# Strassen's identity for the second matrix product of the last 1024 tokens, with a transposed output and weight sums kept in DRAM

## The chip, the cores and the metric

One core of a Trainium2 chip runs the kernel. The metric is the device time of one execution in microseconds (us): 905.93 us before the change (median of three runs, 903.33 to 907.97). TensorE (PE) does the matrix products, VectorE (DVE), ScalarE (ACT) and GpSimd (POOL) the elementwise work, and SyncE (SP) issues nearly all DMAs. Each engine works through its own instructions in order.

## What is computed

```
out_up    = np.repeat(softmax_attention(q_d, k_d, v_d), 4, axis=2)   # means of 4 positions
out_local = softmax_attention(q, k, v, mask |i-j| < 4)
x = (out_up + out_local) as [4608 tokens, 512]
h = x @ w_in                                # w_in  512 x 2048
g = h * np.clip(h + 3.0, 0.0, 6.0) / 6.0
out = g @ w_out                             # w_out 2048 x 512
```

There are 8 batches of 576 positions, so 4608 tokens. The two products are called GEMM1 (with `w_in`) and GEMM2 (with `w_out`). Each 32-bit operand is split into a rounded high part and a rest, and a product is three matmuls: high by high, high by low, low by high. "To round a tile" below means the two instructions that make the parts: one copy (`hi`, mostly ACT) and one subtraction (`lo`, mostly DVE).

## The kernel before

The attention of a batch leaves its part of x in the arena, a large buffer in on-chip memory. The MoE part runs over chunks of 512 tokens (`PART`, nine of them). For chunks 0 to 6 `plan_moe` does GEMM1 block by block (f = 0 to 15, 128 of the 2048 hidden columns each, L1067) and GEMM2 two blocks behind (L1126, accumulated in four PSUM banks o0 to o3, a bank for 128 tokens). While chunk n runs, the attention of the batches of chunk n+1 is worked in between, mostly on DVE, ACT and POOL.

The last two chunks are one piece of 1024 tokens (`plan_strassen`, called with n = `PAIR0` = 7). Their GEMM1 goes by Strassen's identity: for each of eight groups of two hidden blocks, `plan_group` makes sums of the quarters of the weights (`whole` L1333, `mix` L1340, rounded at L1354 and L1357) and seven products P1 to P7 of six matmuls each (L1370) in place of eight. A bank called "chain" takes P1, then P6, P7 and P5 on top, and is copied by ACT in between (L1386); DVE adds the other banks (L1403), and relu and gate follow (L1413, L1417). Their GEMM2 is plain: `plan_parts` rounds each gated tile (L1442 on ACT, L1446 on DVE or POOL) and `gemm2` (L1460) multiplies it. The first chunk's GEMM2 stands between the products of the groups, the second's follows behind all groups. The last tiles leave PSUM in halves (L1032 on ACT, L1034 on DVE) and are stored in pieces of 2 KB rows (L1038) on the queues of SP and ACT.

The order of the instructions is no hand-written list. Every piece of work is declared with `op` (engines and costs, what it waits for, the buffers it takes and frees, a due time `dl`), and `Plan.emit` simulates the engines with a table of costs and writes out each engine's instructions in that order. A lower due time goes first. Work that may go to DVE or POOL goes by cost and by a penalty (`PEN`); with `lock=True` the plan never lets the two run such work at once. On the chip the order is fixed, and only semaphores hold instructions back.

Of the kernel before, what the change touches and what calls it, by code (L numbers as in the profile page):

```python
# [8 lines left out]
F32 = mybir.dt.float32  # L9
# [9 lines left out]
DM, DFF = 512, 2048  # L19
# [37 lines left out]
def tile_local_down_attention_moe(ctx, tc, q_all, k_all, v_all, _qk_loc, _v_loc, w_in, w_out, ident_d, _mask_d, out):  # L57
# [900 lines left out]
    def plan_split(n, prev_last):  # L958
# [3 lines left out]
        def part(i, k, off, cnt):  # L962
            return parts_of(n)[i][:, k:k + ks, off:off + cnt]

        def hi(eng, b, s0, off, cnt, k):
            copy_on(eng, part(0, k, off, cnt), x_of(n, b, k, ks, s0, cnt))

        def lo(eng, b, s0, off, cnt, k):
            eng.tensor_tensor(
                part(1, k, off, cnt), x_of(n, b, k, ks, s0, cnt), part(0, k, off, cnt).bitcast(F32),  # L970
                op=ALU.subtract)
# [36 lines left out]
    def plan_store(n, m, ready, frees):  # L1008
# [9 lines left out]

        def store():
            for p, k, first in stores(at, P):  # L1020
# [4 lines left out]
        if n == len(PART) - 1:  # L1025

            def ev_half(i, eng):
                if i == 0:
                    st_o[n, m] = buf("obz", (n, m), [P, DM])
                cs = slice(i * DM // 2, (i + 1) * DM // 2)  # L1030
                if eng is nc.scalar:
                    eng.activation(st_o[n, m][:, cs], otile[n, m][:, cs], AF.Copy, scale=1.0 / 6.0)  # L1032
                else:
                    eng.tensor_scalar(st_o[n, m][:, cs], otile[n, m][:, cs], 1.0 / 6.0, None, op0=ALU.mult)  # L1034

            def store_half(i, eng):
                for p, k, first in list(stores(at, P))[i::2]:
                    eng.dma_start(  # L1038
                        bass.AP(tensor=out.tensor, offset=out.offset + first, ap=[[32 * DM, k], [1, DM]]),
                        st_o[n, m][p:p + k])  # L1040

            e = [op("ACT", 0.37, partial(ev_half, 0, nc.scalar), [ready], take=[("obz", (n, m))], free=[frees])]
            e.append(op("DVE", 0.37, partial(ev_half, 1, nc.vector), [ready] + e, take=[("obz", (n, m))], free=[frees]))
            op("SP", 1.2, partial(store_half, 0, nc.sync), e, free=[("obz", (n, m))], size=dma(P, 1024), nd=3)
            op("ACT", 1.0, partial(store_half, 1, nc.scalar), e, free=[("obz", (n, m))])
            return
# [3 lines left out]
    def plan_moe(n):  # L1050
# [6 lines left out]
        for f in range(NF):  # L1057
# [49 lines left out]
            read_w[f] = a  # L1107
# [9 lines left out]
        for f in range(NF):  # L1117
# [16 lines left out]
            if f < NF - 1:  # L1134
                before = gemm2
            after = st["ready"] + [w_done["o", f]]
            if n == len(PART) - 1 and f == NF - 2:
                continue
            if n == len(PART) - 1 and f == NF - 1:

                def last_two(m, a=gemm2, b=before):
                    b(m)
                    a(m)

                ops_ = []
                for m in range(parts):
                    ops_.append(op(
                        "PE", 2 * cost, partial(last_two, m), after + gs[f - 1]["ready"] + [w_done["o", f - 1]] + prev[-1:], dl=dl,
                        rec=6))
                    prev.append(ops_[-1])  # L1150
                for key_ in ("gh", "gl"):
                    plan.free_after((key_ + k0, (key_, (n, f - 1))), ops_)
            elif f == 0 or f == NF - 1:
# [27 lines left out]

    def plan_strassen(n, prev_last):

        t0 = start_of(n)
        half = NK // 2
        places = {}
# [17 lines left out]
        def raw_x(t, kh, off, cnt):  # L1204
            b, s0 = divmod((n + t) * TOK + off, S)
            return xt[b][:, kh * half:(kh + 1) * half, s0:s0 + cnt]

        def cuts(*ts):

            at = {0, TOK}  # L1210
            for t in ts:
                at |= {S * b - (n + t) * TOK for b in range(B) if 0 < S * b - (n + t) * TOK < TOK}
            at = sorted(at)
            return [(a, b - a) for a, b in zip(at, at[1:])]

        def ready_x(t, kh, off, cnt):
            b = ((n + t) * TOK + off) // S
            return [x for h in range(kh * half, (kh + 1) * half) for x in x_done[b, h]]
# [3 lines left out]
        def reads(t, off, o):  # L1222
            readers.setdefault(((n + t) * TOK + off) // S, []).append(o)
# [6 lines left out]
        def split(name, source, deps, users, t=None, kh=None):  # L1230

            his, los = [], []
            for off, cnt in cuts(t) if t is not None else [(0, TOK)]:
                def of(off=off, cnt=cnt):
                    return raw_x(t, kh, off, cnt) if t is not None else source()

                def hi(eng, off=off, cnt=cnt, of=of):
                    copy_on(eng, xpart(name, 0)[:, :, off:off + cnt], of())

                def lo(eng, off=off, cnt=cnt, of=of):  # L1240
                    eng.tensor_tensor(xpart(name, 1)[:, :, off:off + cnt], of(),
                                      xpart(name, 0)[:, :, off:off + cnt].bitcast(F32), op=ALU.subtract)

                d = list(deps) + (ready_x(t, kh, off, cnt) if t is not None else [])
# [3 lines left out]
                his.append(a)  # L1248
                los.append(c)
                if t is not None:  # L1250
                    reads(t, off, a)
                    reads(t, off, c)
# [5 lines left out]
        def combine(name, a_of, b_of, deps, cut, frees=()):  # L1258

            got = []  # L1260
            for off, cnt in cut:
                def sub(eng, off=off, cnt=cnt):
                    eng.tensor_tensor(tmp(name)[:, :, off:off + cnt], a_of(off, cnt), b_of(off, cnt), op=ALU.subtract)
                got.append(op(on("xlo", half * cnt), 0, sub, deps(off, cnt), take=[("xT", name)], lock=True))
            return got

        def of_tmp(name):
            return lambda off, cnt: tmp(name)[:, :, off:off + cnt]

        def of_x(t, kh):  # L1270
            return lambda off, cnt: raw_x(t, kh, off, cnt)
# [3 lines left out]
        t1 = combine("t1", of_x(1, 0), of_x(0, 0), lambda o, c: ready_x(1, 0, o, c) + ready_x(0, 0, o, c), cuts(0, 1))  # L1275
        t2 = combine("t2", of_x(1, 1), of_tmp("t1"), lambda o, c: t1 + ready_x(1, 1, o, c), cuts(1))
        split("t2", lambda: tmp("t2"), t2, [])
        t3 = combine("t3", of_x(1, 1), of_x(1, 0), lambda o, c: ready_x(1, 1, o, c) + ready_x(1, 0, o, c), cuts(1))
        split("t3", lambda: tmp("t3"), t3, ["t3"])
        t4 = combine("t4", of_x(0, 1), of_tmp("t2"), lambda o, c: t2 + ready_x(0, 1, o, c), cuts(0))  # L1280
# [12 lines left out]
        loaded, prods, s_free = {}, {}, {}  # L1293
# [4 lines left out]
        def weight(i, j, part, kk):  # L1298
# [7 lines left out]
            pair_, row = {6: (0, 0), 7: (0, 1), 3: (1, 0), 5: (1, 1)}[j]  # L1306
            return sums(part)[:, pair_, row, ks]

        def sums(part):
            return spare(4 + part).rearrange("p k t -> p (k t)").rearrange("p (a r n) -> p a r n", a=2, r=2)  # L1310

        MOVING = {1: "b11", 2: "b21", 3: "b22", 4: "t4", 5: "t1", 6: "t2", 7: "t3"}
        gs = {}

        def plan_group(i):

            at = t0 + GROUP * i
# [11 lines left out]
            def whole(x, eng):  # L1329
                if x == 0:  # L1330
                    st["w"] = buf("wf", i, [P, 2, 512])
                w = blocks(i)[x].bitcast(F32)
                eng.tensor_tensor(st["w"][:, x], w[:, 0], w[:, 1], op=ALU.add)  # L1333

            def mix(k, eng):
                u = st["w"].rearrange("p r (a n) -> p r a n", a=2)
                a11, a12, a21, a22 = u[:, 0, 0], u[:, 0, 1], u[:, 1, 0], u[:, 1, 1]
                out_, x, y, o = ((a22, a21, a22, ALU.add), (a21, a11, a21, ALU.subtract),
                                 (a11, a22, a11, ALU.subtract), (a12, a12, a11, ALU.subtract))[k]
# [686 lines left out]
```

## Time and profile before

| | before |
|---|---|
| median of three runs | 905.93 us |
| the profiled execution | 904.18 us |
| its span, first to last instruction | 902.0 us |
| PE busy in the span | 883.8 us |
| DVE, ACT, POOL busy | 592.2, 472.5, 237.5 us |
| moved by DMA | 106 MB |

The span is shorter than the execution by 2.18 us, which lie outside the first and last instruction. In the rows of the profile "L1460" is line 1460 of the kernel, "PEld" the loading of weights into PE (beside the matmuls), "SPq" and "ACTq" the queues that issue DMAs, and the numbers at the end of a group of instructions are its busy time and the mean of one in ns.

### The profile page before, as it was taken

Reading aid. Unit: us, or ns where it says so; the run is one execution under the profiler, and the core shown is the slowest. Engines: PE = TensorE matmul, PEld = TensorE weight load, DVE = VectorE, ACT = ScalarE, POOL = GpSimd, SP = SyncE. Lnnn points to the kernel's source line nnn. Section 1 sums busy time; section 2 is a strip of 40 time slices with the busy share of each in tenths; the row PEclk is TensorE's granted clock in tenths of the full one; section 3 lists DMA queues with packets and bytes.
Section 4 is the critical chain, followed back from the end, with each engine's and each line's share of the span. In section 5 each row is a group of like instructions: output and inputs, shape, how many; then the busy total and the mean of one; then the engine's idle time right before and its main releaser. Section 6 shows DMA issues by size and latency. Waiting matters only on the chain.

```text
span 902.0 us, 19402 instructions
## 1 busy us (share of the span) xinstructions
PE 883.8 (98%) x6961; PEld 722.2 (80%) x6961; DVE 592.2 (66%) x1073; ACT 472.5 (52%) x1511; POOL 237.5 (26%) x316
## 2 busy tenths in 40 slices
PE   6999999999999999999999999999999999999997
PEld 5667788788888888888888888888888888888886
DVE  7898876466776766656666665666655868766422
ACT  5798866455655455555454535455552334444421
POOL 3655542044522132123211330223110222000000
PEclk9999999999999999999999999999999999999999
DMA  9999843366666663655365546777541022210011
GB/s 227 276 236 235 193 125 70 94 123 120 125 130 125 133 134 72 131 111 114 80 144 103 108 88 136 196 174 190 134 112 36 1 78 86 70 70 24 13 36 47
DMA packets 315759, 106.08 MB, mean 118 GB/s; under 512 B 251792, under 2 KB 298000, under 8 KB 315664
## 3 DMA queue, kind: packets, MB, share of 16 engines
q1 hardware_dynamic: 314384, 103.09, 49.7%
q10 hardware_dynamic: 1280, 1.76, 0.6%
q8 instruction: 55, 0.90, 0.4%
q14 instruction: 40, 0.33, 0.1%
HBM read 75.89 MB, written 28.90 MB: 116 GB/s over the span
## 4 chain that ended last, share of the span: by engine, by line
PE 90%; DMA 3%; DVE 2%; SPq 2%; ACT 1%; issue 0%; POOL 0%; ACTq 0%; DVEq 0%
PE o L1126 33%; PE h L1067 31%; PE o L1460 5%; PE a L1370 5%; PE h L1370 4%; PE a L1460 2%; PE h L1460 2%; PE a L709 2%; PE h L752 2%; PE a L501 1%; PE h L664 1%; DMA early<-in_v_dram 1%; DMA arena<-in_k_dram 1%; DMA out_dram<-arena 1%; SPq L323 0%; DMA arena<-in_q_dram 0%
## 5 line engine op out<-in xcount | busy, mean ns | idle before, releaser
L1126 PE MATMUL o<-wp,rounded 128*128 128x512 f32 x1344 | 324.1, 393 | 2.7 <-DVE arena L1017 1.6
L1067 PE MATMUL h<-rounded,wp 128*128 128x512 f32 x1344 | 316.9, 390 | 1.2 <-DVE arena L1077 1.0
L1067 PEld LDWEIGHTS h<-rounded,wp 128*128 128x128 f32 x1344 | 251.3, 188 | 54.8 <-DVE arena L1077 1.4
L1126 PEld LDWEIGHTS o<-wp,rounded 128*128 128x128 f32 x1344 | 249.5, 188 | 56.8 <-DVE arena L1017 2.0
L1077 DVE SCALAR_TENSOR_TENSOR arena<-arena,h 128x512 f32<-128x512 f32 x112 | 76.0, 679 | 61.8 <-ACT arena L1073 61.3
L1085 DVE TENSOR_TENSOR rounded<-arena,rounded 128x512 fp32r<-128x512 f32 x85 | 61.9, 730 | 72.0 <-PE o L1126 54.2
L1073 ACT ACTIVATE arena<-h 128x512 f32<-128x512 f32 x112 | 66.6, 594 | 78.8 <-PE h L1067 76.2
L1081 ACT CAST rounded<-arena 128x512 fp32r<-128x512 f32 x112 | 68.9, 615 | 73.9 <-PE o L1126 44.1
L565 ACT ACTIVATE arena<-arena 128x64 f32<-128x64 f32 x240 | 80.2, 337 | 0.5
L422 POOL TENSOR_TENSOR arena<-arena 32x256 f32<-32x256 f32 (+1 forms) x26 | 22.3, 858 | 117.0 <-DMA arena<-in_v_dram 116.9
L1085 POOL TENSOR_TENSOR rounded<-arena,rounded 128x512 fp32r<-128x512 f32 x27 | 35.9, 1331 | 63.9 <-PE o L1126 45.1
L329 DVE STREAM_TRANSPOSE arena<-arena 128x576 f32<-128x576 f32 x56 | 43.2, 771 | 12.7 <-DMA arena<-in_q_dram 6.3
L1460 PE MATMUL o<-wp,rounded 128*128 128x512 f32 x192 | 49.2, 389 | 0.0
L378 POOL TENSOR_TENSOR arena<-arena 128x144 f32<-128x144 f32 x33 | 14.9, 450 | 128.2 <-DVE arena L329 50.0
L565 ACT ACTIVATION_READ_ACCUMULATOR arena<-arena 128x1 f32 x240 | 45.2, 188 | 0.0
L1460 PEld LDWEIGHTS o<-wp,rounded 128*128 128x128 f32 x192 | 36.0, 188 | 7.5
L684 ACT ACTIVATE arena<-h 128x144 f32<-128x144 f32 x24 | 7.0, 290 | 66.2 <-PE h L664 66.2
L380 POOL TENSOR_TENSOR arena<-arena 128x144 f32<-128x144 f32 x66 | 38.7, 586 | 5.2
L541 ACT ACTIVATE arena<-arena 128x1 f32<-128x1 f32 (+1 forms) x78 | 15.0, 193 | 43.5 <-DVE arena L554 43.4
L1370 PE MATMUL a<-wp,wp 128*128 128x512 f32 x150 | 37.2, 389 | 0.0
L1446 DVE TENSOR_TENSOR rounded<-arena,rounded 128x512 fp32r<-128x512 f32 x27 | 18.6, 690 | 26.8 <-PE h L1460 21.1
L420 DVE TENSOR_REDUCE arena<-arena 128x128 f32<-128x512 f32 (+1 forms) x26 | 27.6, 1065 | 12.9 <-PE h L664 10.8
(240 smaller groups left out, 1239.9 us busy)
## 6 DMA issues: line engine op xcount, KB each, us to landing
rawp<-in_w_in_dram SPq DMA_DIRECT2D x16, 512.0 KB
rawp<-in_w_out_dram SPq DMA_DIRECT2D x16, 512.0 KB
arena<-in_q_dram SPq DMA_DIRECT2D x112, 72.0 KB
arena<-in_k_dram SPq DMA_DIRECT2D x112, 72.0 KB
pl<-arena SPq DMA_DIRECT2D x24, 320.0 KB
arena<-pl SPq DMA_DIRECT2D x96, 80.0 KB
arena<-in_v_dram SPq DMA_DIRECT2D x28, 256.0 KB
out_dram<-arena SPq DMA_DIRECT2D x89, 72.0 KB
```

Of the source, the lines that this page charges most:

```text
L329: nc.vector.transpose(out=qk[kind], in_=qk[kind])
L380: eng.tensor_tensor(t, t, x[:, :, r], op=ALU.add)
L420: eng.tensor_reduce(out=vd, in_=raw.rearrange("p r e -> p e r"), op=ALU.add, axis=AX.X)
L565: nc.scalar.activation(x[:, j], x[:, j], AF.Exp, bias=m[:, j:j + 1], scale=0.125, accum_out=s[:, j:j + 1])
L1067: nc.tensor.matmul(st["ps"], win[f][:, wt, kk * P:(kk + 1) * P], xs[part][:, kk], start=(kk == 0 and i == 0), stop=(kk == NK - 1 and i == ...
L1073: nc.scalar.activation(st["t"], st["ps"], AF.Relu, bias=3.0)
L1077: nc.vector.scalar_tensor_tensor(out=t, in0=t, scalar=6.0, in1=st["ps"], op0=ALU.min, op1=ALU.mult)
L1081: nc.scalar.copy(st["gh"], st["t"])
L1085: eng.tensor_tensor(st["gl"], st["t"], st["gh"].bitcast(F32), op=ALU.subtract)
L1126: nc.tensor.matmul(otile[n, m], gt[:, ms], wout[f][:, wt], start=(f == 0 and i == 0), stop=(f == NF - 1 and i == 2),)
L1370: nc.tensor.matmul(ps, weight(i, j, wt, kk), xpart(MOVING[j], part)[:, kk], start=first and kk == 0 and x == 0, stop=kk == half - 1 and x ...
L1460: nc.tensor.matmul(otile[n + t, m], gt[:, ms], wout[f][:, wt], start=f == 0 and x == 0, stop=f == NF - 1 and x == 2)
```

## The change

GEMM2 of the last 1024 tokens is also done by Strassen's identity. The gated activations G and `w_out` are each cut in quarters, a pair of hidden blocks giving the two halves of the inner dimension, and seven products of the quarters' sums take the place of eight. The weights are now the stationary operand and the activations the moving one, so the output is accumulated transposed (output columns by tokens).

- *Sums of the weights.* `plan_sum` makes the sums for both products while chunks 2 to 6 run (32 pieces, `SUMS_AT`): six instructions on POOL or DVE for a piece, and one DMA that keeps it in DRAM. The piece lies in a slot of the buffer `ob`, in which output tiles wait for their store. The groups no longer make sums; they load them (`load_s`).
- *The groups.* P1 and P2 of GEMM2 need the two gated tiles g11 and g21 alone and stand between the products of GEMM1 (`unit`, four steps of three matmuls a group). The four differences of gated tiles (`diff`) that the other products need are made in the group and put into DRAM, but for the first one and those of the last group, which stay in the arena.
- *The last stage.* `plan_units` runs the other five products one after another, P5, P6, P3, P7, P4, with 48 matmuls each. Its 16 weight tiles and 40 activation tiles go through a ring of 20 places (`RING`: the places of GEMM1's operands, as these come free); 44 of them are loaded from DRAM, and all are rounded in place.
- *The output.* `finish` adds the accumulators on DVE and turns each tile of 128 columns by 512 tokens with DVE's transposition of 32x32 blocks. `plan_out` stores it in runs of 32 columns, 128 bytes each, with a late due time (`t1 + 60`).
- *Tokens.* So that a block of 32 turned tokens lies at a fixed step in the output, the 1024 tokens are all of batch 7 and most of batch 6, in another order; chunk 6 takes the first 128 tokens of batch 6 in that order. Relu and gate now hold the factor 1/6.

```diff
+    def plan_sum(n, f, kind, i, h):
...
+        o = [op(on("s256", 1), 0, partial(whole, x), [w_done[kind, 2 * i + x], gemm1_of[n, f]], take=[("so", un)], lock=True) for x in range(2)]
+        for k in range(4):
+            o = [op(on("s128", 1), 0, partial(mix, k), o, lock=True)]
+        to["ops"].append(op("SP", 0.5, put, o, free=[("so", un)], size=dma(4 * P, 512), dl=start_of(n) + TF * (f + 4) * TOK / SHARE))
...
-            ws = [op(on("s512", 1), 0, partial(whole, x), [ld[x]] + ld[2:], take=[("wf", i)], lock=True) for x in range(2)]
...
+                o = op("SP", 0.5, partial(load_s, a), sums_in[i]["ops"], take=[("sr", (i, a))], size=dma(P, 2048))
...
+            d1 = diff("g11", "g12", "g11", [gated["g12"], rounds["g11"]])
+            d2 = diff("t2", "g22", "g11", [gated["g22"], d1])
+            d3 = diff("g12", "g22", "g12", [gated["g22"], d1])
+            d4 = diff("g21", "g21", "t2", [rounds["g21"], d2])
...
+            for j, m, pos in ((1, 0, 2), (1, 1, 4.5), (2, 0, 7), (2, 1, 7.5)):
...
+        RING = (0, 1, 6, 7, 8, 9, 10, 11, 14, 15, 12, 13, 18, 19, 16, 17, 2, 3, 4, 5)
...
+            o = op("SP", 0.5, fill, list(deps) + free_, size=dma(P, 2048))
+            o = op(on("zhi", TOK), 0, hi, [o])
+            rounded_op[key] = op(on("zlo", TOK), 0, lo, [o], lock=True)
...
+            if name in ENDS:
+                a = op("DVE", 0.7, add, ready, free=frees)
+                o = op("DVE", 0.75, turn_, [a])
...
+                    eng.dma_start(bass.AP(tensor=out.tensor, offset=at + EDGE * DM, ap=[[32 * DM, 32], [DM, NC - EDGE], [1, 32]]),
+                                  x[:, :NC - EDGE])
+                    eng.dma_start(bass.AP(tensor=out.tensor, offset=at + LONG * 32 * DM, ap=[[DM, 32], [32 * DM, RP - LONG], [1, 32]]),
+                                  x[:, NC - EDGE:])
+            last_ = dict(dl=t1 + 60.0)
...
+        "so": slots["ob"][:1],
```

How this stands on the engines at three places. The first is PE at the very end of the program; before, the rows are the last two hidden blocks of the second chunk's GEMM2, a bank at a time (a and h are PSUM banks, "rounded" the rounded activations, wp weights):

```order
L1460 MATMUL a_9116<-wp_1743,rounded 128x512 x3
L1460 MATMUL a_9116<-wp_1746,rounded 128x512 x3
L1460 MATMUL a_9122<-wp_1743,rounded 128x512 x3
L1460 MATMUL a_9122<-wp_1746,rounded 128x512 x3
L1460 MATMUL h_9126<-wp_1743,rounded 128x512 x3
L1460 MATMUL h_9126<-wp_1746,rounded 128x512 x3
L1460 MATMUL h_9130<-wp_1743,rounded 128x512 x3
L1460 MATMUL h_9130<-wp_1746,rounded 128x512 x3
```

Now there stand the last matmuls of P7 and, from the fifth row on, the start of P4, in the two banks o_8606 and o_8645:

```order
L1632 MATMUL o_8606<-wp_1249,wp_1137 128x512 x3
L1632 MATMUL o_8645<-wp_1110,wp_980 128x512 x3
L1632 MATMUL o_8645<-wp_1225,wp_1137 128x512 x3
L1632 MATMUL o_8645<-wp_1249,wp_1137 128x512 x3
L1632 MATMUL o_8606<-wp_1440,wp_891 128x512 x3
L1632 MATMUL o_8606<-wp_1534,wp_983 128x512 x3
L1632 MATMUL o_8645<-wp_1440,wp_891 128x512 x3
```

Four banks are replaced by two that P7 and P4 share; before P4 may write a bank, DVE has to have read P7's result out of it.

The second place is the end of SP's queue. Before, it is the last stores of 2 KB rows:

```order
L1021 DMA out_dram<-arena 28x512
L1038 DMA out_dram<-arena 8x512
L1038 DMA out_dram<-arena 36x512
L1038 DMA out_dram<-arena 12x512
L1038 DMA out_dram<-arena 24x512
```

Now it is the last loads of the ring (g_ are activation tiles in DRAM) and then the stores of the turned tiles:

```order
L1521 DMA rounded<-g_4_9069 128x512
L1521 DMA rounded<-g_6_9338 128x512
L1521 DMA rounded<-g_5_9168 128x512
L1596 DMA out_dram<-arena 32x16x32 x4
L1598 DMA out_dram<-arena 32x12x32
L1600 DMA out_dram<-arena 32x4x32
```

All 40 stores of turned tiles on this queue stand behind the last of the 44 loads; the pair L1598 and L1600 comes 16 times, and four L1596 end the queue.

The third place is the end of DVE's instructions in the changed kernel (L1527 is the `lo` of a loaded tile, L1567 an addition of `finish`, L1570 and L1583 the turning):

```order
L1527 TENSOR_TENSOR wp_1318<-wp_1318 128x512
L122 CAST wp_1249<-arena 128x512
L1567 TENSOR_TENSOR arena<-o_8675,arena 128x512
L1567 TENSOR_TENSOR arena<-o_8683,arena 128x512
L1567 TENSOR_TENSOR arena<-h_9311,arena 128x512
L1567 TENSOR_TENSOR arena<-a_9315,arena 128x512
L1570 STREAM_TRANSPOSE arena<-arena 128x512 x4
L1527 TENSOR_TENSOR rounded<-rounded 128x512
L1567 TENSOR_TENSOR arena<-o_8606,arena 128x512
L1570 STREAM_TRANSPOSE arena<-arena 128x512
L1567 TENSOR_TENSOR arena<-o_8645,arena 128x512
L1570 STREAM_TRANSPOSE arena<-arena 128x512
```

Before, DVE ended with the four evictions L1034. Now the first finished outputs (o_8675 and o_8683, complete early in the last stage) are added and turned here, behind nearly all of the rounding; the four halves of transposition L1583 end the list. Until the second group of the GEMM1 by Strassen, PE's own order is the same in both kernels.

More of the change, by code (lines that the diff above doesn't have):

```diff
@@ L1133, in plan_moe @@
             g, parts, cost = gemm2, nm, 0.683
-            if f < NF - 1:
-                before = gemm2
             after = st["ready"] + [w_done["o", f]]
[L1137 to L1153, printed above, removed]
+            if f == 0 or f == NF - 1:
                 ops_ = []
@@ L1185, in plan_strassen @@
         half = NK // 2
+        NG = NF // 2
         places = {}
@@ new lines, in plan_group @@
+            for name, x, done, frees in (
+                    ("g11", lambda: st["a"], c11, [tcs["a"]]), ("g21", lambda: st["c"], c21, [tcs["c"]]),
+                    ("g22", chain, p5, [("hp", (i, "chain"))]), ("g12", lambda: st["b"], c12, [tcs["b"]])):
+                r = op("ACT", 0.6, partial(relu, name, x, toks[name]), [done], take=[toks[name]])
+                gated[name] = op("DVE", 0.68, partial(gate, name, x), [r], free=frees)
+            plan.free_after(("hp", (i, "chain")), [e])
@@ new lines, in unit @@
+            def unit(j, m):
+                key = "o%d" % (2 * (j - 1) + m)
+                if i == 0:
+                    places[j, m] = bank(key, n)
+                name = ("g11", "g21")[j - 1]
+                w = wout[2 * i + j - 1]
+                for x, (wt, part) in enumerate(((0, "h"), (0, "l"), (1, "h"))):
+                    nc.tensor.matmul(places[j, m], w[:, wt, m * P:(m + 1) * P], st[name, part], start=i == 0 and x == 0, stop=i == NG - 1 and x == 2,
+                                     skip_group_check=True)
@@ new lines, in plan_strassen, with take, run, finish @@
+        ENDS = "p1", "u2", "p5"
+        ACCS = {5: "z", 6: 1, 3: "z", 7: 1, 4: 1}
+        t1 = t0 + 9 * UNIT * NG + 2 * UNIT
+        ends = {(1, m): halves[1, m, last] for m in range(2)}
+        copies = {}
+        def take(name, acc, m, ready):
+            def run():
+                copies[name, m] = buf("ts", (name, m), [P, TOK])
+                nc.scalar.copy(copies[name, m], places[acc, m])
+            return op("ACT", 0.6, run, ready, take=[("ts", (name, m))])
+        def finish(name, acc, m, ready, mh, t, frees=()):
+            M = 2 * mh + m
+            def add():
+                nc.vector.tensor_tensor(copies[name, m], places[acc, m], copies[name, m], op=ALU.add)
+            def turn_():
+                nc.vector.transpose(out=copies[name, m], in_=copies[name, m])
+            tok = [("ts", (name, m))]
+            if name in ENDS:
+                a = op("DVE", 0.7, add, ready, free=frees)
+                o = op("DVE", 0.75, turn_, [a])
+                plan_out(lambda: copies[name, m], M, t, [o], tok)
+                return a
+            def turn_half(i):
+                if i == 0:
+                    copies[name, m] = buf("ts", (name, m), [P, TOK])
+                ks = slice(i * TOK // 2, (i + 1) * TOK // 2)
+                nc.vector.transpose(out=copies[name, m][:, ks], in_=places[acc, m][:, ks])
+            o = [op("DVE", 0.45, partial(turn_half, i), ready, take=tok) for i in range(2)]
+            plan_out(lambda: copies[name, m], M, t, o, tok)
@@ new lines, in plan_strassen @@
+        c1 = [take("p1", 1, m, [ends[1, m]]) for m in range(2)]
+        for m in range(2):
+            finish("p1", 2, m, [c1[m], halves[2, m, last]], 0, 0, [("o%d" % (2 + m), n)])
+        plan_units(5, {})
+        c5 = [take("p5", "z", m, [ends[5, m]]) for m in range(2)]
+        plan_units(6, {m: [c1[m]] for m in range(2)})
+        u2 = [take("u2", 1, m, [ends[6, m]]) for m in range(2)]
+        plan_units(3, {m: [c5[m]] for m in range(2)})
+        for m in range(2):
+            finish("u2", "z", m, [ends[3, m], u2[m]], 0, 1, [("hp", ("z", m))])
@@ L1507, in tile_local_down_attention_moe @@
+        plan_units(7, {m: [u2[m]] for m in range(2)}, 1)
+        done = [finish("p5", 1, m, [ends[7, m], c5[m]], 1, 1) for m in range(2)]
+        plan_units(4, {m: [done[m]] for m in range(2)}, 2)
+        for m in range(2):
+            finish("u3", 1, m, [ends[4, m]], 1, 0)
     spilled = {}
```

453 lines of the change are left out of this document (268 added, 185 removed).

## The prediction

> **What bounds the kernel now.** I read the page's busy shares first, then its slices and the chain that ended last, then busy time by stretches.
>
> ```profile
> PE 883.8 (98%) x6961; PEld 722.2 (80%) x6961; DVE 592.2 (66%) x1073; ACT 472.5 (52%) x1511; POOL 237.5 (26%) x316
> PE   6999999999999999999999999999999999999997
> PEclk9999999999999999999999999999999999999999
> PE 90%; DMA 3%; DVE 2%; SPq 2%; ACT 1%; issue 0%; POOL 0%; ACTq 0%; DVEq 0%
> ```
>
> PE is busy in every slice but the first and last, at the full granted clock, and it is 90% of the chain. The stretches (columns: length, then busy us and count for PE, PEld, DVE, ACT, POOL, then clock, DMA share, GB/s) show the same for the middle and for the last 1024 tokens:
>
> ```profile
> 200.00:300.00 100.00, 100.00 (x929) 83.01 (x929) 67.39 (x126) 55.98 (x231) 37.95 (x55) 1.00 0.63 125
> 720.00:760.00 40.00, 40.00 (x178) 33.14 (x177) 30.37 (x44) 17.29 (x30) 11.20 (x8) 1.00 0.25 79
> 840.00:880.00 40.00, 40.00 (x179) 33.10 (x178) 13.66 (x20) 13.37 (x23) 1.29 (x1) 1.00 0.10 27
> ```
>
> A full PE can still be waiting between pipelined matmuls, so I take the pace from starts:
>
> ```profile
> 891.07 2.88 PE L1460 MATMUL a<-wp,rounded 128*128 128x512 f32 x12
> 893.79 2.88 PE L1460 MATMUL h<-wp,rounded 128*128 128x512 f32 x12
> ```
>
> Twelve matmuls start in 893.79 - 891.07 = 2.72 us: 0.2267 us each, gapless. So in the last stage nothing but PE sets the time, and removed matmuls count in full unless something else becomes late.
>
> **Term 1, matmuls.** GEMM2 of 1024 tokens was 2 x 16 blocks x 4 banks x 3 = 384 matmuls; now it is 7 products x 8 pairs x 2 halves x 3 = 336, with the same 128x512 shape. 48 x 0.2267 = **-10.9 us**. GEMM1 keeps its 336.
>
> **Term 2, weight sums in chunks 2 to 6.** By the order, DVE gets 47 additions of 128x256 and 71 of 128x128, POOL 17 and 57.
>
> ```profile
> L1340 DVE TENSOR_TENSOR arena<-arena 128x256 f32<-128x256 f32 x23 | 9.8, 425 | 4.4 <-POOL arena L1340 3.8
> L1340 POOL TENSOR_TENSOR arena<-arena 128x256 f32<-128x256 f32 x9 | 8.9, 985 | 71.2 <-DVE arena L1333 71.1
> L1263 DVE TENSOR_TENSOR arena<-arena 128x128 f32<-128x128 f32 x1 | 0.3, 284 | 0.0
> L378 POOL TENSOR_TENSOR arena<-arena 128x144 f32<-128x144 f32 x33 | 14.9, 450 | 128.2 <-DVE arena L329 50.0
> 172.90 6.42 PE L1126 MATMUL o<-wp,rounded 128*128 128x512 f32 x27 [1.57 <-DVE arena L1017]
> ```
>
> DVE: 47 x 0.425 + 71 x 0.284 = 40 us; POOL, with the 128x144 row for the small ones: 17 x 0.985 + 57 x 0.45 = 42 us. Spread over some 550 us that lifts DVE from 67% to about 75% and POOL from 38% to 45%; PE's work covers it. What could uncover it is the last row: at one change of chunk PE waited 1.57 us for an output tile to leave PSUM, and the sums now hold one of the two slots that these tiles go through. The ends are 0 and one such wait at each of five changes, 7.9 us; the sums are declared mostly in the middle of a chunk, so I take 0.3.
>
> **Term 3, the groups.** A group was 42 matmuls of GEMM1 and, behind the first, 24 of GEMM2; now it is 42 + 12 = 54, 12.2 us. DVE gets about 107 of the 128x512 instructions in eight groups (counted in the order), ACT some 88:
>
> ```profile
> L1403 DVE TENSOR_TENSOR arena<-a,arena 128x512 f32<-128x512 f32 x12 | 8.2, 686 | 4.8 <-PE a L1370 4.8
> L1386 ACT COPY arena<-a 128x512 f32<-128x512 f32 x15 | 8.8, 587 | 26.2 <-PE a L1370 26.2
> L1446 POOL TENSOR_TENSOR rounded<-arena,rounded 128x512 fp32r<-128x512 f32 x1 | 1.3, 1286 | 32.0 <-PE o L1460 32.0
> ```
>
> DVE 107 x 0.686 = 73 us of 98 (75%, as 30.37 of 40 before), ACT 55%, POOL 29 x 1.286 = 37 us. The tightest chain is P1, ACT's copy, P6: the gap on PE is P2 and one step, 2.04 us, for 0.587 and two hand-overs; before, a gap of 1.36 us (P6 to P7) cost no idle time. I take 0; the ends are 0 and 1 us.
>
> **Term 4, feeding the last stage.** Its 240 matmuls last 54.4 us and need 56 tiles: 44 loads, 56 copies, 56 subtractions. In P6, P3 and P7, 12 tiles go into 10.9 us, 0.91 us each.
>
> ```profile
> L1442 ACT CAST rounded<-arena 128x512 fp32r<-128x512 f32 x28 | 17.3, 622 | 28.0 <-PE h L1460 18.3 <-DVE arena L1417 8.7 <-PE o L1460 1.0
> L1446 DVE TENSOR_TENSOR rounded<-arena,rounded 128x512 fp32r<-128x512 f32 x27 | 18.6, 690 | 26.8 <-PE h L1460 21.1 <-ACT rounded L1442 3.4 <-PE o L1460 2.1
> 733.00:745.00 12.00, 12.00 (x55) 9.93 (x54) 6.13 (x10) 5.89 (x11) 1.36 (x2) 1.00 0.57 173
> ```
>
> ACT takes 0.622, DVE 0.690, and the DMAs, which in a stretch of 2 KB stores moved 173 GB/s at a share of 0.57 (303 GB/s when full), 262144 B / 303 = 0.87 us. All keep up, the DMAs barely; the ring's 20 places give 18 us of lead. The thin spot is the start. When GEMM1's last product is done, DVE still has eight instructions by the order (two additions, two gates, two copies, two `lo`) before the fifth tile of the stage's first product is ready: 8 x 0.690 = 5.5 us and some 0.4 of hand-overs. PE needs that tile 36 matmuls after that moment, at 8.2 us. That leaves 2.3 us. POOL's differences fall into the same time, and the two engines disturb each other:
>
> ```profile
> 705.46 2.40 POOL L1263 TENSOR_TENSOR arena<-arena 128x1024 f32<-128x1024 f32 x1 [0.90 <-DVE arena L757]
> 705.48 3.47 DVE L1263 TENSOR_TENSOR arena<-arena 128x1024 f32<-128x1024 f32 x1
> 710.27 1.21 DVE L1241 TENSOR_TENSOR wp<-arena,wp 128x1024 fp32r<-128x1024 f32 x1
> ```
>
> Beside a POOL subtraction the DVE one took 3.47 us, alone 1.21: it stood still for nearly all of POOL's 2.40. Two POOL differences in that time cost 2 x 1.286 = 2.6 us, just past the slack; seven in series cost 9.0 - 2.3 = 6.7. Ends 0 and 6.7; I take 1.0.
>
> **Term 5, P7 to P4.** P4 accumulates onto the bank that P7 ends in, so PE waits for DVE's addition; behind PE's waiting instruction the rest of P4 is queued. For the second half the order leaves two steps, 1.36 us, for 0.686 and two hand-overs, which fits if DVE is there. By the third place of the order, DVE first has a copy, four additions and four transpositions, 6.1 us. They stand behind a `lo` whose place P3's sixth tile frees 24.6 us before PE's end; with some 4.6 us to load, copy and subtract (estimated from 0.87 above, a landing of about 2, and 0.622 and 0.690) they start at about -20 and end at -14. The first addition for P7 is due at -13.0. Ends 0 and 2; I take 0.5.
>
> **Term 6, the output.** The transpositions:
>
> ```profile
> L329 DVE STREAM_TRANSPOSE arena<-arena 128x576 f32<-128x576 f32 x56 | 43.2, 771 | 12.7 <-DMA arena<-in_q_dram 6.3 <-DMA arena<-in_k_dram 6.1
> L631 DVE STREAM_TRANSPOSE arena<-arena 128x384 f32<-128x384 f32 x24 | 13.7, 571 | 0.0
> 894.97 0.42 DVE L1034 TENSOR_SCALAR arena<-a 128x256 f32<-128x256 f32 x1 [1.50 <-ACT arena L1032]
> 897.55 0.42 DVE L1034 TENSOR_SCALAR arena<-h 128x256 f32<-128x256 f32 x1 [1.36 <-ACT arena L1032]
> 898.01 0.83 ACTq L1038 DMA_DIRECT2D out_dram<-arena  x2
> L323 SPq DMA_DIRECT2D arena<-in_q_dram x112: 311/497/3263, 23.2 to 624.5; - x112
> L616 SPq DMA_DIRECT2D arena<-pd x96: 303/460/1749, 142.5 to 676.0; - x96
> L621 SPq DMA_DIRECT2D arena<-pd x96: 397/427/1792, 144.4 to 678.0; - x96
> ```
>
> From 576 and 384 columns, 256 columns take 0.43 us. Before, PE's last matmul ends at 893.79 + 2.88 = 896.67, DVE's last eviction at 897.97, and the span at 902.0: 5.3 us, 4.03 of them for issue and landing. Now DVE ends some 0.2 + 2 x 0.43 = 1.1 us behind PE, with one more issue of about 0.1 us and more packets: 5.3 us again, if SP is free. SP has 40 stores to issue. Issues of 576, 384 and 96 short packets took 0.50, 0.46 and 0.43 us, so a pair (384 and 128) is about 0.88, 16 pairs 14.1, the first four 2.0. The first tile is turned some 15 us before PE's end (term 5: a copy, two to four additions and a transposition from -20 on), so SP comes to the last four stores some 1 us behind it, as late as DVE turns the last tile, and with two tiles to store instead of one. I take +1.5; ends 0 and 5.
>
> The Trainium skill (DMA: Bandwidth & Descriptors, Specifications) says that transfers under 512 bytes miss line rate because the DMA engine reads, modifies and writes. It speaks against this output, whose runs are 128 bytes; no row here shows such a store, and by that rule the last rival below would be the forecast.
>
> **Sum.** 904.18 - 10.9 + 0.3 + 1.0 + 0.5 + 1.5 = 896.6 us for the profiled execution. This one lies 1.75 us below the median of its three runs, which differ by 4.6 us; I move the sum up a little, to **897.0**.
>
> **Rivals.**
> *The feed starts late* (term 4's upper end): DVE and POOL take turns behind the last group, PE waits for its fifth to eighth tile of P5. For it speaks the 3.47 us row; against it that the plan keeps marked work of the two apart. 896.6 - 1.0 + 6.7 = 902.3.
> *The sums cost what was gained* (term 2's upper end): PE waits at every change of chunk. For it the wait of 1.57 us at 172.90, against it that the other changes of before show none. 896.6 - 0.3 + 7.9 = 904.2.
> *The short stores are slow*, the side on which the change loses. The nearest row is a stretch of reads in runs of 128 and 64 bytes:
>
> ```profile
> 143.00:148.00 5.00, 5.00 (x24) 4.14 (x23) 4.84 (x8) 3.33 (x10) 1.58 (x1) 1.00 0.33 44
> ```
>
> 44 / 0.33 = 133 GB/s, so 128 bytes hold one of 16 engines 15.4 ns. The output is 16384 such packets: 16384 / 16 x 15.4 ns = 15.8 us, which fits beside the last 15 us of PE and the tail. At twice that, 31.5 us, the engines end 16.5 us behind PE and the tail is about 18.5 us instead of 6.8: 896.6 + 11.7 = 908.3. It loses against before (a tail of 14.4 us) from about 1.75 times 15.4 ns on, and is slower by 0.5% from about twice on.
>
> **How the numbers follow.** A measurement of this kernel tells about 0.5% (4.5 us) from no change. Forecast (893.5 to 900.5): 0.72. Late feed: 0.10, half of it beyond 901.4 us and so no change. Sums: 0.08, no change. Slow stores: 0.10, half no change, half slower. Faster 0.77, same 0.18, slower 0.05. The range runs from 892.5, no loss anywhere, to 904.0, which takes in the late feed, part of the sums' case and leaves the slow stores out.
>
> **What would show it.** Term 1: 240 matmuls on L1632 and 96 on L1484 at 0.2267 us. Term 2: no new waits of PE before 700 us. Terms 4 and 5: idle time of PE before L1632, at the fifth to eighth tile of P5, or between P7 and P4. Term 6: how long the span goes on behind the last matmul, and whether SP's last issues wait for DVE or only for each other. The forecast is wrong if PE's idle time in the last stage passes 5 us or the tail 10 us.

## The result and the profile after

| | before | after |
|---|---|---|
| median of the runs compared | 903.37 us (20 runs) | 898.89 us (20 runs) |
| ratio, 95% interval | | 0.9948, 0.9936 to 0.9961 |
| the profiled execution | 904.18 us | 897.61 us |
| its span | 902.0 us | 895.8 us |
| behind PE's last matmul | 5.3 us | 8.9 us |
| moved by DMA | 106 MB | 138 MB |

The change is faster by half a per cent, within the range and 1.9 us above the forecast of 897.0. The page's busy shares, its slices of PE, and the chain that ended last:

```profile
PE 874.8 (98%) x6913; PEld 714.5 (80%) x6913; DVE 667.9 (75%) x1226; ACT 489.3 (55%) x1542; POOL 304.4 (34%) x397
PE   7999999999999999999999999999999999999996
PE 87%; DVE 5%; DMA 2%; ACT 2%; SPq 1%; issue 1%; POOL 0%; DVEq 0%
```

PE has 48 matmuls fewer (6913 for 6961) and is still what the chain runs over, but its last digit fell from 7 to 6: the span now goes on longer without PE. One stretch at the end of the last group (length, then busy us and count of PE, PEld, DVE, ACT, POOL, clock, DMA share, GB/s) shows where it is tight:

```profile
820.00:840.00 20.00, 18.94 (x81) 14.64 (x80) 19.90 (x24) 13.40 (x25) 10.77 (x8) 1.00 0.73 239
```

Between 820 and 840 us, DVE has no time left (19.90 of 20) and PE is idle for 1.06 us, which it never was in this part before. The timeline of PE, first before, at the first matmuls of the stage:

```profile
727.87 1.52 PE L1370 MATMUL a<-wp,wp 128*128 128x512 f32 x6
```

and after, there, at the end of the last group, and at the end:

```profile
726.99 1.52 PE L1374 MATMUL a<-wp,wp 128*128 128x512 f32 x6
...
824.91 1.52 PE L1484 MATMUL o<-rounded,wp 128*128 128x512 f32 x6
826.46 1.66 PE L1374 MATMUL a<-rounded,wp 128*128 128x512 f32 x6
827.95 0.39 PE L1484 MATMUL o<-rounded,wp 128*128 128x512 f32 x1
829.27 1.42 PE L1484 MATMUL o<-rounded,wp 128*128 128x512 f32 x5 [0.93 <-DVE rounded L1442]
830.52 0.86 PE L1632 MATMUL h<-wp,wp 128*128 128x512 f32 x3
...
864.99 16.48 PE L1632 MATMUL o<-wp,wp 128*128 128x512 f32 x72
881.31 5.60 PE L1632 MATMUL o<-rounded,wp 128*128 128x512 f32 x24
```

From these starts the whole difference can be put together:

- Up to the first P1: 726.99 - 727.87 = -0.9 us.
- From there to PE's last end (896.67 before, 881.31 + 5.60 = 886.91 after): 168.80 us before, 159.92 after, 8.9 less. The 48 matmuls are 10.9 us, so **2.0 us are lost to waits**. From 824.91 to 830.52 stand 18 matmuls, 4.08 us, in 5.61: 1.5 us of it. The bracket alone (0.93) would have missed a third of that; the starts show it.
- Behind PE: 902.0 - 896.67 = 5.3 before, 895.8 - 886.91 = 8.9 after: **3.6 us lost**.

-10.9 - 0.9 + 2.0 + 3.6 = -6.2 us, which is the difference of the spans.

What DVE and POOL did before the wait (timelines of both, after):

```profile
821.99 0.68 DVE L1407 TENSOR_TENSOR arena<-h,arena 128x512 f32<-128x512 f32 x1
...
823.43 1.78 DVE L1421 SCALAR_TENSOR_TENSOR first<-first,arena 128x512 f32<-128x512 f32 x1
825.13 1.78 DVE L1527 TENSOR_TENSOR wp<-wp 128x512 fp32r<-128x512 f32 x1
826.83 1.78 DVE L1542 TENSOR_TENSOR wp<-arena,wp 128x512 fp32r<-128x512 f32 x1
828.53 0.68 DVE L1442 TENSOR_TENSOR rounded<-first,rounded 128x512 fp32r<-128x512 f32 x1
```

```profile
823.18 1.48 POOL L1452 TENSOR_TENSOR first<-arena 128x512 f32<-128x512 f32 x1
824.62 1.74 POOL L1452 TENSOR_TENSOR arena<-arena 128x512 f32<-128x512 f32 x1
826.33 1.74 POOL L1452 TENSOR_TENSOR first<-first 128x512 f32<-128x512 f32 x1
```

The `lo` at 828.53 is the tile that PE waits for. The three instructions before it take 1.78 us each beside POOL's differences, where alone they take 0.68.

The tail (timelines of DVE and of SP's queue, after):

```profile
886.95 0.78 DVE L1583 STREAM_TRANSPOSE first<-o 128x256 f32<-128x256 f32 x2 [0.58 <-PE o L1632]
```

```profile
871.46 2.26 SPq L1596 DMA_DIRECT2D out_dram<-arena  x4
873.99 0.68 SPq L1598 DMA_DIRECT2D out_dram<-arena  x1
...
875.62 0.44 SPq L1598 DMA_DIRECT2D out_dram<-arena  x1
876.10 0.49 SPq L1600 DMA_DIRECT2D out_dram<-arena  x1
876.64 0.44 SPq L1598 DMA_DIRECT2D out_dram<-arena  x1
...
891.43 0.91 SPq L1596 DMA_DIRECT2D out_dram<-arena  x2
892.44 1.00 SPq L1596 DMA_DIRECT2D out_dram<-first  x2
```

DVE has turned the last tile at 887.73, but SP is busy with its 16 pairs until 891.43 and issues the last store until 893.44. Most issues last 0.44 to 0.49 us, but the pairs start about 1.02 us apart (0.94 to 1.14, and 1.63 and 1.55 at two jams): between two issues stand another 0.04 to 0.10 us that no duration holds. In the middle of these pairs the DMA engines were less than half busy (columns as above: DMA share 0.43, 66 GB/s):

```profile
880.00:882.00 2.00, 2.00 (x11) 1.65 (x10) 0.00 (x0) 0.00 (x0) 0.00 (x0) 1.00 0.43 66
```

### The profile page after: what moved, and what is told of

Its sections match the earlier page's. It is cut to its first block, busy times and chain, and to the rows that moved or that the text cites. A ratio compares the mean times of both kernels' runs of the same rounds, so it can differ in the third digit from the quotient of the medians.

```text
span 895.8 us, 19863 instructions
## 1 busy us (share of the span) xinstructions
PE 874.8 (98%) x6913; PEld 714.5 (80%) x6913; DVE 667.9 (75%) x1226; ACT 489.3 (55%) x1542; POOL 304.4 (34%) x397
## 4 chain that ended last, share of the span: by engine, by line
PE 87%; DVE 5%; DMA 2%; ACT 2%; SPq 1%; issue 1%; POOL 0%; DVEq 0%
PE o L1119 33%; PE h L1060 31%; PE a L1374 4%; PE o L1632 4%; PE h L1374 3%; PE a L709 2%; PE o L1484 2%; PE h L752 2%; PE a L501 1%; PE h L664 1%; PE h L1632 1%; PE a L1632 1%; DMA early<-in_v_dram 1%; DMA arena<-in_k_dram 1%; DMA arena<-in_q_dram 0%
## 5 line engine op out<-in xcount | busy, mean ns | idle before, releaser
L1119 PE MATMUL o<-wp,rounded 128*128 128x512 f32 x1344 | 324.2, 393 | 2.2 <-DVE wp L202 1.1
L1119 PEld LDWEIGHTS o<-wp,rounded 128*128 128x128 f32 x1344 | 249.6, 188 | 56.2 <-DVE wp L202 1.6
L1078 DVE TENSOR_TENSOR rounded<-arena,rounded 128x512 fp32r<-128x512 f32 x83 | 61.7, 746 | 43.6 <-PE o L1119 34.3
L1078 POOL TENSOR_TENSOR rounded<-arena,rounded 128x512 fp32r<-128x512 f32 x29 | 39.0, 1345 | 70.8 <-PE o L1119 45.6
L1182 POOL TENSOR_TENSOR arena<-arena 128x128 f32<-128x128 f32 x57 | 28.9, 506 | 76.3 <-DVE arena L1182 42.4
L378 POOL TENSOR_TENSOR arena<-arena 128x144 f32<-128x144 f32 x30 | 13.5, 450 | 110.5 <-DVE arena L329 74.5
L380 POOL TENSOR_TENSOR arena<-arena 128x144 f32<-128x144 f32 x60 | 35.3, 588 | 4.7
L582 DVE TENSOR_TENSOR arena<-arena 128x640 f32<-128x640 f32 (+1 forms) x43 | 35.8, 834 | 1.1
L1374 PE MATMUL a<-wp,wp 128*128 128x512 f32 x138 | 34.2, 389 | 0.0
L423 POOL TENSOR_TENSOR arena<-arena 32x128 f32<-32x128 f32 (+1 forms) x27 | 14.5, 536 | 49.2 <-PE h L664 37.5
```

Of the source, the lines that this page charges most:

```text
L380: eng.tensor_tensor(t, t, x[:, :, r], op=ALU.add)
L582: eng.tensor_tensor(x, x, s.unsqueeze(2).broadcast_to(list(x.shape)), op=ALU.mult)
L1078: eng.tensor_tensor(st["gl"], st["t"], st["gh"].bitcast(F32), op=ALU.subtract)
L1119: nc.tensor.matmul(otile[n, m], gt[:, ms], wout[f][:, wt], start=(f == 0 and i == 0), stop=(f == NF - 1 and i == 2),)
L1374: nc.tensor.matmul(ps, weight(i, j, wt, kk), xpart(MOVING[j], part)[:, kk], start=first and kk == 0 and x == 0, stop=kk == half - 1 and x ...
```

## The experiments

"The changed kernel" is the one above; run once more beside the first experiments (`again`), it took 898.17 us, ratio 0.9939 (0.9917 to 0.9961). The experiments ran on three chips: `again`, two_queues, long_runs and diffs_dve on one, two_queues_long and the three early ones on the second, lock, lock_order and no_mix on the third. The kernel before was timed on each (904.00, 902.62 and 903.24 us), so across chips the ratios to it are compared and not the times.

> The changed kernel itself, beside the others on one chip. Every theory: 897 to 900 us and a ratio of 0.993 to 0.997 to the kernel before, with PE's last matmul some 8.9 us ahead of the span's end.

**Two queues for the stores.**

```diff
-                if q < 2 or t:
+                if q < 2:
                     op("SP", 0.5, partial(store, nc.sync, (q,)), ...)
+                elif t:
+                    op("ACT", 1.1, partial(store, nc.scalar, (q,)), ...)
```

> The second two quarters of each long tile are stored by ACT's queue instead of SP's: SP has 24 stores of turned tiles left in place of 40. Theory 1, SP's issues set the tail (16 pairs at 1.08 us each from 874 us on): SP is through with the long tiles some 8 us earlier, before PE's end, and behind the last matmul stand 0.8 us of turning, two issues of 0.5 and a landing of 2.4: a tail of 4.2 to 5.3 us in place of 8.9, 894.5 to 896 us, 3 to 4.5 less than the changed kernel. Theory 2, the 128-byte runs themselves set it (the DMA engines are not through with them): the same packets take as long, tail 8 to 9 us, 898 to 900 us.

894.30 us, ratio 0.9895 (0.9873 to 0.9917), 3.9 us less than the changed kernel on the same chip. Timelines of PE and of both queues:

```profile
880.89 5.60 PE L1634 MATMUL o<-rounded,wp 128*128 128x512 f32 x24
887.34 0.87 SPq L1596 DMA_DIRECT2D out_dram<-first  x2
887.35 0.96 ACTq L1596 DMA_DIRECT2D out_dram<-first  x2
```

The last stores are issued as soon as DVE has turned them (887.31), the last issue ends at 888.31 and the span at 892.2. PE ends at 880.89 + 5.60 = 886.49: a tail of 5.7 us in place of 8.9 (8.2 in `again`), and the same 2.0 us lost before it (first P1 at 726.56, so 159.93 us). Theory 1 holds; 5.7 is a little above what it expected.

**Long runs on one queue, then on two.** Here the 1024 tokens are left out of the output.

```diff
-                        eng.dma_start(bass.AP(tensor=out.tensor, offset=at + NC * DM, ap=[[32 * DM, 32], [DM, NC], [1, 32]]), x)
+                        eng.dma_start(d, x)          # d: a scratch in DRAM, [32, 16, 32]
...
```

> The 1024 tokens are left out of the output: the same number of stores with the same bytes write the turned tiles to a scratch in DRAM, in runs of 512 bytes to 2 KB. Theory 1 (SP's issues): an issue took 0.44 us with 384 short runs and 0.47 with 128, so their number and pace stay: tail 8 to 9 us, 898 to 900 us. Theory 2 (the short runs): the packets fall from 16384 to 1536, tail 5 to 6 us, 895 to 896 us.

895.36 us, ratio 0.9904 (0.9883 to 0.9926): 2.8 us less, where theory 1 expected none and theory 2 about 3. By its timelines neither holds as it was put:

```profile
882.29 5.60 PE L1630 MATMUL o<-rounded,wp 128*128 128x512 f32 x24
877.71 0.43 SPq L1598 DMA_DIRECT2D fat<-arena  x1
878.18 0.42 SPq L1599 DMA_DIRECT2D fat<-arena  x1
890.66 0.84 SPq L1596 DMA_DIRECT2D fat<-first  x2
```

SP's queue is still what ends last (its last issue ends at 891.50, PE at 887.89), but two issues now start 0.47 us apart, 0.93 a pair instead of 1.02, and the tail is 5.8 us. With fewer packets the issues themselves came faster, so this run changes both suspects. The next one doesn't:

> Stores on two queues as in two_queues, and the 1024 tokens left out of the output: the turned tiles go to a scratch in DRAM in runs of 512 bytes to 2 KB. What is left of the tail in two_queues is 5.7 us, in which the DMA engines were full for 2 us and 0.85 full for 2 more, at 140 GB/s. Theory, with the issues spread the 128-byte packets of the last 512 KB (3.7 us at 140 GB/s) set the end: longer runs take under 2 us, tail 4.0 to 4.6, 892.5 to 893.5 us. Rival, issue and landing alone set it: tail 5.5 to 5.9, 894 us as two_queues.

893.50 us, ratio 0.9891 (0.9868 to 0.9915), which can't be told from the 0.9895 of two_queues; what follows rests on one trace of each. PE, ACT's queue and the stretch from 0.3 to 2.3 us behind PE's end, then a stretch of two_queues from 1.5 to 3.5 us behind its own:

```profile
880.14 5.60 PE L1632 MATMUL o<-rounded,wp 128*128 128x512 f32 x24
886.60 1.16 ACTq L1596 DMA_DIRECT2D fat<-first  x2
886.00:888.00 2.00, 0.00 (x0) 0.00 (x0) 0.56 (x2) 0.00 (x0) 0.00 (x0) 1.00 0.79 216
```

```profile
888.00:890.00 2.00, 0.00 (x0) 0.00 (x0) 0.00 (x0) 0.00 (x0) 0.00 (x0) 0.96 1.02 143
```

With long runs the tail is 890.0 - 885.74 = 4.3 us, 1.4 less than two_queues. So by the traces the tail of the changed kernel has two layers: SP's issues on top (2.5 to 3.2 us), and below them the 128-byte packets of the last tiles (1.4 us), which show only once the queue is out of the way.

**The differences of the last group on DVE alone.**

```diff
-                return op(on("sg", 1), 0, partial(minus_, to, x, y), ...)
+                return op({"DVE": (0.72, 0.0)} if i == NG - 1 else on("sg", 1), 0, partial(minus_, to, x, y), ...)
```

> The four differences of the last group go to DVE alone. Theory A, DVE and POOL disturb each other there (DVE's instructions of 0.4 and 0.68 us took 1.5 to 1.8 us beside POOL's between 819 and 829 us, 6 us lost in all): these go back to 0.4 and 0.7, DVE gains 6 us and pays 4 x 0.69 = 2.8, PE's wait of 0.93 us before the last group's P2 and most of the 2.0 us that PE loses between the first P1 and its end go: 1 to 2 us less than the changed kernel. Theory B, DVE simply has too much to do in these 10 us: with 2.8 us more the wait grows to 2 to 4 us, and the time by 1 to 3 us.

901.32 us, ratio 0.9974 (0.9959 to 0.9989), 3.2 us slower than the changed kernel, and not for either reason. (The profiled execution is the slowest of its twelve, 905.29 us: its first P1 comes 4.4 us later than in the profile after. The reading below is taken from PE's end.) The differences beside which DVE was slow belong to the group before the last, so the edit missed them, and PE's wait of 0.94 us stayed. Instead the plan put the turning of the first tiles later (SP's queue):

```profile
879.41 2.27 SPq L1596 DMA_DIRECT2D out_dram<-arena  x4
900.14 1.00 SPq L1596 DMA_DIRECT2D out_dram<-first  x2
```

SP's first store stands 11.5 us before PE's end (890.95) where it was 15.5 in the profile after, 3.9 us later, and the tail grew from 8.9 to 12.6 us, by 3.7. For the contention this run tells nothing; for the tail it is a second witness: what comes late into SP's queue comes late out of it, nearly one for one.

**The first tiles earlier, and then the contention, both with two queues.**

```diff
-            last_ = dict(dl=t1 + 60.0)
+            last_ = dict(dl=t1 + (60.0 if M > 1 else 40.0))
```

> On top of two_queues the first half of the output columns is added, turned and stored with a due time 20 us earlier. If nothing but the packets and issues of the last tiles is left in the tail, nothing is gained: 893.8 to 894.8 us. If stores of earlier tiles still held the engines when the last ones came, the tail falls from 5.7 to about 5: 893.5 us. If DVE's additions and transpositions now stand in the way of the rounding, PE shows new waits in the last 25 us and the time is 895 or more.

898.71 us, ratio 0.9942 (0.9923 to 0.9961): by its time the third of the three outcomes, though only one of its new waits lies in the last 25 us. PE, then DVE and POOL:

```profile
840.79 0.73 PE L1634 MATMUL h<-wp,wp 128*128 128x512 f32 x2 [1.21 <-DVE wp L1542]
879.58 5.74 PE L1634 MATMUL o<-wp,wp 128*128 128x512 f32 x24 [0.64 <-DVE arena L1567]
```

```profile
838.98 1.76 DVE L1542 TENSOR_TENSOR wp<-arena,wp 128x512 fp32r<-128x512 f32 x1
838.58 1.61 POOL L1452 TENSOR_TENSOR arena<-arena 128x512 f32<-128x512 f32 x1
```

From first P1 to PE's end it takes 161.96 us, 4.0 lost in place of 2.0; the tail is 5.7 as in two_queues. One loss is another `lo` beside POOL in P5, the other the hand-over from P7 to P4, which the changed kernel does not show. (Another 2.2 us of the time stand before the first P1, where the order is the same; see below.)

> On top of early, all differences of gated tiles in the last two groups go to DVE (eight in place of two). Theory A, DVE and POOL disturb each other between 819 and 829 us: DVE's copies, gates and subtractions go back from 1.5 to 1.8 us to 0.4 to 0.7 (6 us), DVE pays some 6 x 0.69 = 4.1 us, the wait of 0.93 us before L1484 and most of the 2.0 us lost from the first P1 to the end go: 1 to 2 us less than early. Theory B, DVE has too much to do there: the wait grows to 2 to 4 us, 1 to 3 us more than early.

Its edit is that of diffs_dve with `i >= NG - 2`. 902.59 us, ratio 0.9995 (0.9977 to 1.0013). PE and DVE:

```profile
835.01 1.65 PE L1634 MATMUL a<-wp,wp 128*128 128x512 f32 x3 [4.32 <-DVE arena L1407]
830.94 1.75 DVE L1410 TENSOR_TENSOR arena<-arena 128x512 f32<-128x512 f32 x1
```

Theory B's number (166.79 us to PE's end, 4.8 more than early), but not quite its reason: DVE has the extra work, and the slow instructions stayed too, because the plan filled POOL with `lo`s in the differences' place. Moving one kind of work does not end the contention.

> On top of early the plan also keeps the gates and DVE's copies in the last stage from running beside POOL's work; no instruction changes its engine by the edit itself, only by the plan. Theory A (the two disturb each other): fewer DVE instructions over 1 us between 805 and 840, PE's losses there fall from 2.0 to below 1: 1 to 1.5 us less than early. Theory B (too much work in all, or the order on the chip slips out of the plan's anyway): as early within 0.5 us, or more, with DVE waiting for POOL's turns.

```diff
-                gated[name] = op("DVE", 0.68, partial(gate, name, x), [r], free=frees)
+                gated[name] = op("DVE", 0.68, partial(gate, name, x), [r], free=frees, lock=True)
...
-            o = op(on("zhi", TOK), 0, hi, [o])
+            o = op(on("zhi", TOK), 0, hi, [o], lock=True)
...
```

894.76 us, ratio 0.9901 (0.9881 to 0.9921): 158.91 us to PE's end, 3.1 less than early, as theory A has it and more; between 805 and 840 us five DVE instructions last over 1 us where early has ten. `lock` is the same with a due time of 44 in place of 40:

> two_queues plus the plan keeping gates and DVE's copies away from POOL's work, and the first half of the output columns due only 16 us earlier, so that the additions for P7 stay in time. From first P1 to PE's end early_lock lost 1.0 us in place of 2.0, 0.3 of it at P7 to P4. If DVE and POOL's contention was the loss and the early finishing the rest: 0.7 to 1.0 us lost, 1.0 to 1.3 less than two_queues, 0.988 to 0.9885 of the kernel before. If early_lock's gain was of the lock only against early's own mistake: as two_queues, 0.9895.

894.64 us, ratio 0.9900 (0.9879 to 0.9922). One PE row has what is left of the loss at the end of the last group, 0.34 us:

```profile
829.15 1.86 PE L1484 MATMUL o<-rounded,wp 128*128 128x512 f32 x6
830.85 1.53 PE L1634 MATMUL a<-wp,wp 128*128 128x512 f32 x6
```

From first P1 (728.51) to PE's end (886.78) it takes 158.27 us, 0.35 above the 157.92 of a gapless PE; two_queues lost 2.0. So keeping DVE's gates and copies off POOL's work takes away 1.7 us of the loss. The plan also moves work with it, from POOL to DVE. The stretch from the first P1 on, two_queues and then lock (columns as above):

```profile
728.00:830.00 102.00, 101.04 (x445) 83.03 (x444) 84.97 (x112) 51.94 (x93) 38.93 (x27) 1.00 0.61 194
728.00:830.00 102.00, 101.95 (x450) 84.10 (x450) 80.62 (x124) 53.13 (x96) 20.28 (x14) 1.00 0.60 191
```

In lock DVE does twelve instructions more and is busy 4.35 us less, with POOL at half its work. That speaks against a mere surplus of work on DVE and for the contention; as the order changed too, it is not shown that contention alone made the loss. By the time of the whole program lock is no faster than two_queues (0.9900 against 0.9895).

> On top of lock, P4's last four steps go first to one bank and then to the other (so far the last two): the first bank of the last pair is done 2.7 us before PE's end in place of 1.36. If the 128-byte packets of the last 512 KB set the tail (3.7 us at 140 GB/s), 1.36 us of them move in front of PE's end: tail 4.5 to 5.0 in place of 5.7, 0.7 to 1.2 us less than lock. If issue and landing of the very last stores set it: as lock.

```diff
-both[3:-2] + one[-2:] + two[-2:] if by_part else both
+both[3:-4] + one[-4:] + two[-4:] if by_part else both
```

895.39 us, ratio 0.9910 (0.9886 to 0.9934), with a profiled execution of 892.89 us, the shortest of the kernels that compute everything. PE and SP's queue:

```profile
880.34 5.60 PE L1634 MATMUL o<-rounded,wp 128*128 128x512 f32 x24
886.79 0.85 SPq L1596 DMA_DIRECT2D out_dram<-arena  x2
```

Its tail is 891.1 - 885.94 = 5.2 us for lock's 5.7: less than the packets' theory gave (0.7 to 1.2), and too little to be seen in the time.

**The weight sums.**

```diff
-        for k in range(4):
-            o = [op(on("s128", 1), 0, partial(mix, k), o, lock=True)]
+            pass
```

> Left out are four of the six instructions of each of the 32 pieces of weight sums in chunks 2 to 6 (57 on POOL and 71 on DVE): the last 1024 tokens come out of wrong sums. If the sums cost PE time before 700 us (the wait of 1.1 us for DVE's L757 at 606 us and the one of 1.0 for an output tile at 170 us): both go and the time falls by 1 to 2 us, to 896.5 to 898 us. If they lie beside PE's work: waits of this kind stay, and the time is that of the changed kernel, 898 to 899.5 us.

896.66 us, ratio 0.9940 (0.9914 to 0.9966), the ratio of the changed kernel (0.9939 and 0.9948): what the sums cost is too little to be seen in the program's time. The traces tell more. The first sum starts at 272.06 us in the changed kernel, so the wait of 1.0 us at 170 us can't come from the sums; no_mix has it too (1.1 us). Between the first sum and the first P1, PE's waits in the chunks (us in all, times, longest) and what DVE did ahead of L757, the instruction waited for, are in the changed kernel:

```profile
PE h L1060 <- DVE first L757: 1.1, 1, 1.1
606.89 0.94 DVE L1182 TENSOR_TENSOR arena<-arena 128x128 f32<-128x128 f32 x3
```

and the waits in no_mix:

```profile
PE h L1060 <- DVE arena L757: 0.3, 1, 0.3
```

The kernel before has 0.2 us there. L757 adds a result of the attention out of a PSUM bank; in the changed kernel DVE works five instructions of the sums (L1177 and L1182, 1.8 us) in the 4.2 us before it, while PE comes to need the bank. From the first product of chunk 2 to the first P1 it takes 483.25 us in the changed kernel, 482.04 in no_mix and 481.97 before; in eleven executions with all the sums it is 482.3 to 484.2, with a median of 483.4. So the sums do not lie wholly beside PE's work. By one trace each of a kernel without them and of one with a third of their instructions, they cost about 1 us (0.3 to 2.3 in the eleven).

## Why the prediction came out as it did

**Term 1 was right.** 48 matmuls are gone, at 0.2267 us.

**Term 2 (sums, +0.3) was sized too small: +1.3.** The engines' work came out as forecast (DVE 41.2 us for 40, POOL 43.5 for 42, DVE's share of the stretch 73% for 75%), but it was not all covered: from the first product of chunk 2 to the first P1 the changed kernel takes 1.3 us more than before, 1.1 of it the wait for L757 above. That is not the wait the term was built on: the one for an output tile lies ahead of the first sum. The -0.9 us in front of the first P1 comes of an earlier start: chunk 2 begins at 243.74 us in the profile after and at 245.90 before, 2.2 us apart. That is mostly scatter: in eleven executions with one order up to there, chunk 2 begins between 243.5 and 248.0 us and the first P1 between 725.8 (two_queues_long) and 731.4 (diffs_dve, whose granted clock was 0.93 in its first 50 us; without it, up to 245.3 and 729.6). Whether a part of the 2.2 us belongs to the change is open. The scatter is as large as the effects sought, which is why times to PE's end are taken from the first P1.

**Term 3 (groups, 0) was wrong by 1.5 us, and term 4 (feeding, +1.0) cost 0.5.** The mechanism, DVE standing still beside POOL, is that of term 4's 3.47 us row; it struck in the last groups and not behind them, at the second unit product (L1484). The step that failed is the count in term 3: DVE at 75% of a group's 12.2 us, worked out from undisturbed durations. From 740 to 820 us it is busy for 71.1 of 80 us, 89%, and in the stretch 820 to 840 for 99.5%. The plan's `lock` was taken as protection, but gates and copies don't carry it, and what carries it slips out of the planned times on the chip. The Trainium skill (SBUF — State Buffer, Who interferes with whom) says which DVE instructions contend with POOL: those with two inputs in SBUF, the memory that holds the arena, and those in a mode with two ports, but not those with at most one such input outside that mode. The rows agree: L1407 at 821.99, which reads one operand from PSUM, took 0.68 us beside a POOL instruction, the gate and the `lo`s 1.78.

**Term 5 (P7 to P4, +0.5) cost nothing here**, PE runs gapless from 864.99 on; in early, where DVE's order differs, the 0.64 us of this very wait appear.

**Term 6 (output, +1.5) was right in mechanism and mis-sized: +3.6.** SP's queue is the tail, as stated, but a pair was put at 0.88 us from the durations of the issues, and takes 1.02 from start to start. The right figure stood in the trace of before, in the starts (SP's timeline):

```profile
302.83 1.98 SPq L616 DMA_DIRECT2D arena<-pd  x4
304.92 1.82 SPq L621 DMA_DIRECT2D arena<-pd  x4
```

Four issues of L616 in 304.92 - 302.83 = 2.09 us are 0.52 each; over the whole trace the median step is 0.51 behind L616 and 0.47 behind L621, 0.98 a pair. For PE the prediction took starts, for SP durations. By the pace alone 16 pairs take 2.2 us more than 14.1, and two jams add 1.1: they took 17.4 us (873.99 to 891.43), so that SP came to the last four stores 4.5 us behind PE and not about 1.

**The rivals.** The late feed did not come, and of the sums' cost about 1 us of the 7.9. The short stores were not slow in the rival's sense: 143 GB/s at a share of 1.02 (two_queues) are 128 bytes in 14.6 ns per engine, no more than the 15.4 of the reads it was reckoned from. The Trainium skill (DMA: Bandwidth & Descriptors, Specifications) has transfers under 512 bytes below line rate; the long runs' 216 GB/s at 0.79, 273 when full, agree with that.

**The sum** was 896.6 for the profiled execution; it took 897.61. The terms missed by +1.0 (2), +0.5 (3 to 5) and +2.1 (6); -2.2 lies ahead of chunk 2, and -0.4 lies outside the span (2.18 us before, 1.81 after). That the sum came within 1.0 us is thus partly luck: the early start hid some 2 of the 3.6 us by which the terms were short. The gain in the medians, 4.5 us, is smaller than the 6.6 of the profiled executions; the scatter above is large enough for that, and no other cause was looked for.

## What to carry to other kernels

A queue's pace is read from the starts of its issues, not from their durations, and here a late queue was paid behind the last matmul nearly in full: count the issues that remain when the last tile is ready, and spread them before anything else. An engine that is 75% busy by undisturbed durations can be full in the stretch that matters, if its neighbour stops it; work both engines' overlap into the count. Work that fits beside the busiest engine on average can still stand in front of the one instruction that it waits for, as the sums did. And the version to keep here is two_queues, a change of a few lines: 894.3 us, ratio 0.9895; what lock and lock_order gain in the trace on top of it could not be told from the scatter of the times.

## What the runs showed of the hardware

- A store of 384 runs of 128 bytes is not dearer to issue than one of 128 (0.44 and 0.47 us), but with runs of 512 bytes and more (long_runs) both took 0.42, and the time between starts fell from 0.51 to 0.46 us (medians): the number of packets does reach back into the issuing queue.
- A store of 128-byte runs holds a DMA engine for 14.6 ns a run (two_queues), less than loads in runs of 128 and 64 bytes did (15.4 per 128 bytes, before).
- Splitting the same stores over two queues took 2.5 to 3.2 us off the tail (8.2 and 8.9 to 5.7 us); in the middle of the long queue the DMA engines were 0.43 busy.
